# Attention ahead of two expert layers: k's maximum over slots in a PSUM bank, router columns with heads innermost, and a new order of tasks

## The chip, the cores and the metric

The kernel runs on one core of a Trainium2 chip. The core has five engines that take their instructions from queues of their own: TensorE (PE, the matrix engine), VectorE (DVE), ScalarE (ACT), GpSimd (POOL) and SyncE (SP, which here only issues DMAs). They share SBUF and the eight banks of PSUM, and meet through semaphores. The metric is the device time of one execution in microseconds, lower is better.

## What is computed

Linear attention over 8 batches of 8 heads, 576 positions and 64 columns, whose output is the input of two layers of experts (a top-1 router and eight experts each). The change touches the attention alone.

```python
def _attn_ref(q, k, v) -> np.ndarray:
    q_s = q - np.max(q, axis=-1, keepdims=True)
    q_s = np.exp(q_s)
    q_s = q_s / (np.sum(q_s, axis=-1, keepdims=True) + 1e-09)
    k_s = k - np.max(k, axis=2, keepdims=True)
    k_s = np.exp(k_s)
    k_s = k_s / (np.sum(k_s, axis=2, keepdims=True) + 1e-09)
    kv = np.einsum('bhsd,bhse->bhde', k_s, v)
    return np.einsum('bhsd,bhde->bhse', q_s, kv).astype(np.float32)

def reference(**kwargs):
...
    attn_out = _attn_ref(**attn_kwargs)
    B, H, S, D = attn_out.shape
    x = np.ascontiguousarray(attn_out.transpose(0, 2, 1, 3)).reshape(B * S, H * D)
    x = _moe_ref(x=x, **moe_kwargs)
    return _moe2_ref(x=x, **moe2_kwargs)
```

The maximum of k runs over the 576 positions, so it needs a maximum over slots on each partition and then one across partitions. Each expert layer sends a row of 512 to the expert with the largest logit; the first one leaves rows with a score of zero or less as they are.

## The kernel before

**Tiling.** The 576 positions of a batch are 512 in the main part, position 4p + j on partition p in slot j (NB = 4 slots), and 64 in a rest, which is slot 4 (NS = 5 slots). k lies in SBUF as `kt` [128, 8 heads, 5 slots, 64], two buffers for eight batches; v likewise as `vt`, q as `qt` with its rests as `qr` for two batches at a time.

**k's maximum** is made in `do_k` in two halves g of four heads. L191 (DVE) reduces over slots with the slot as the innermost index of a rearranged view, a step of 64 elements, and writes `m1`. PE transposes it into a bank of the pool `p1` (L193), DVE reduces over what were partitions (L195), ACT spreads the result to 128 columns (L196), PE transposes back into a second bank (L198). Then ek = k - maximum: on DVE straight from the bank in the batches listed under `kV` (L202), else on POOL from a copy that ACT makes (L204, L205). ACT takes the exponential (L206) and copies v beside a column of ones (`vp`, L207). PE multiplies (L216), which gives the product and the sum; L220 to L229 scale it into `KV`, on ACT in the batches of `nA`, else on DVE. L235 to L242 append to `KV` the 17 columns of the routers (8 and 8 logits and the score), so that the output and the routers' columns come out of one product.

**q and the output.** `do_q` subtracts each position's maximum (L251 on DVE; L252 on POOL, or on DVE in batches of `qV`) and takes the exponential. `do_out` transposes each slot (L270), multiplies by `KV` (L285), and DVE divides by the sum: the output into `xb` (L292), the 17 columns of each head into `lp` (L293), which lies as [slot, head, 17]. `place` sums `lp` over the heads (L314), finds the expert by some ten small DVE steps, counts places by PE (L325 to L327), and POOL scatters the rows to the array X in HBM (L344), 36 scatters in all. Eight batches make ten such units, the last two batches being cut in two.

**What sets the order.** Every piece is a task with a priority, a price for each engine that may run it, and the values it reads and writes (`sch.add`). `Order.emit` goes through time with these prices: it takes the ready task that can start first (within a window) and then by priority, gives it a buffer of its pool, and so writes a fixed order of instructions for every engine, the loads on SP among them. Priorities are batch x `step` plus an offset for the kind of task (`off`) and one for kind and batch (`ob`), from the table PRM. The pool `p1` has four PSUM banks, used for all transposes and small products; `po` has two.

**Behind it** the first expert layer splits its weights in two parts (L503 on ACT; L504 in turn on DVE and POOL) and runs its products at L534 and L564.

Of the kernel before, what the change touches and what calls it, by code (L numbers as in the profile page):

```python
# [94 lines left out]
def attention(tc,nc,raw,ctx,cst,q,k,v,routers,wgt,enD,X,accF,w1,w2,early,prm={}):  # L95
# [10 lines left out]
    def mk(name,shape,n,pool=None,dt=F32): pools[name]=[(pool or wk).tile(shape,dt,name=f"{name}{i}") for i in range(n)]  # L106
# [6 lines left out]
    mk('xb',[128,NS,XW],nb['xb'],raw); mk('lp',[128,NS,H,17],1)  # L113
# [67 lines left out]
    def do_k(b):  # L181
# [28 lines left out]
        for a in range(2):  # L210
# [19 lines left out]
            add(u+2*a+2,dict(A=1.0) if b in prm.get('nA',()) else dict(V=.5),f,[pk,ks],[(KV,a)])  # L230
        m=n; NC2=4//m
        for a in range(m):
# [10 lines left out]
            add(u+6,dict(A=.45) if b in prm.get('nA',()) else dict(V=.3),f,[p4],pt(KV,m,a))  # L243
    def do_q(b):
# [4 lines left out]
        for g in range(n):  # L249
            js=slice(NJ*g,NJ*g+NJ)  # L250
            add(u,dict(V=2.13/n+.07),lambda e,js=js: V.tensor_reduce(out=x.tile[:,:,js],in_=qt.tile[:,:,js],axis=AX.X,op=ALU.max),[qt],pt(x,n,g))  # L251
            add(u+.5,dict(V=2.13/n+.07) if fast else dict(P=4.4/n),lambda e,js=js: E[e].tensor_tensor(out=eq.tile[:,js].rearrange("p j h d -> p h j d"),in0=qt.tile[:,:,js],in1=x.tile[:,:,js].unsqueeze(3).to_broadcast([128,H,NJ,D]),op=ALU.subtract),[qt]+pt(x,n,g),pt(eq,n,g))  # L252
            add(u+1,dict(A=1.73/n+.07),lambda e,js=js: A.activation(out=eq.tile[:,js],in_=eq.tile[:,js],func=AF.Exp),[],pt(eq,n,g))
        if b%2:
            y=val(('qy',i))
            add(u,dict(V=.6),lambda e: V.tensor_reduce(out=y.tile,in_=qr.tile,axis=AX.X,op=ALU.max),[qr],[y])
            add(u+.5,dict(P=1.2),lambda e: P.tensor_tensor(out=qr.tile,in0=qr.tile,in1=y.tile.unsqueeze(2).to_broadcast([128,H,D]),op=ALU.subtract),[y],[qr])
            add(u+1,dict(A=.52),lambda e: A.activation(out=qr.tile,in_=qr.tile,func=AF.Exp),[],[qr])
    def do_out(b):
# [41 lines left out]
    def place(key,nj,xk,lk,xt,lt,prio,ids):  # L301
# [12 lines left out]
        add(prio,dict(V=.06+.145*nj),lambda e: V.tensor_reduce(out=l(),in_=lt().rearrange("p j h n -> p j n h"),axis=AX.X,op=ALU.add),lk,[ls])  # L314
# [543 lines left out]
```

## Time and profile before

| what | us |
|---|---|
| median of 3 runs (1058.69 to 1059.56) | 1058.87 |
| the profiled execution | 1061.93 |
| its span, first to last instruction | 1060.1 |
| attention, first instruction to the last DVE step of the routers' order | 0 to 176.0 |
| expert layers | from there to 1060.1 |

| engine, whole span | busy us | share |
|---|---|---|
| PE | 966.6 | 91% |
| DVE | 612.7 | 58% |
| ACT | 462.0 | 44% |
| POOL | 410.3 | 39% |

The shares are means over stages that have different limits: behind 176 us PE has the most work by far, in the attention PE and DVE are close. So the attention has to be read by itself: by the busy time in stretches, by the groups of instructions within 0 to 176.4 us, and by the waits. A group's row gives the source line, the engine, the operation, output and inputs by name, shapes, the count, the busy time in us and the mean duration in ns; after the bar the time that the engine stood idle just before them, and who ended it. Durations of one engine overlap a little where instructions follow each other without depending on each other, so that busy time is less than the sum of durations.

### The profile page before, as it was taken

How to read it: one execution, taken by the hardware profiler on the slowest of the kernel's cores; microseconds unless marked ns; L12 is line 12 of the kernel's file. 1: busy time of each engine (PE TensorE's matmuls, PEld its weight loads, DVE VectorE, ACT ScalarE, POOL GpSimd, SP SyncE). 2: the span in 40 equal slices, each digit the busy share in tenths (PEclk: the TensorE clock that was granted, in tenths of full speed). 3: DMA queues.
4: the chain of work that ended last, by engine and by line, in shares of the span. 5: the costliest groups of instructions: out<-in, count | busy, mean ns of one | idle time of the engine just before them, and what ended most of it. 6: DMA issues, size and time to landing. Idle time of an engine off the chain costs nothing. (4 is left out here: it accounts for less than half of the span.)

```text
span 1060.1 us, 19802 instructions
## 1 busy us (share of the span) xinstructions
PE 966.6 (91%) x6075; PEld 861.2 (81%) x6075; DVE 612.7 (58%) x1552; ACT 462.0 (44%) x945; POOL 410.3 (39%) x363
## 2 busy tenths in 40 slices
PE   4888987798899999999998899999999999999994
PEld 3777986786689977878996789889888899998893
DVE  6999877776466775766676621271634422255360
ACT  5877654125526252262225413273534332455352
POOL 6476846106958347273213711031401300134040
PEclk9999998899899999999999989999999999999998
DMA  9989725551653316233111372051341710063500
GB/s 289 317 249 321 251 95 208 194 182 41 226 165 113 119 62 204 89 121 123 49 54 54 120 265 72 32 205 58 117 142 40 250 43 22 22 217 114 171 29 22
DMA packets 88635, 144.76 MB, mean 137 GB/s; under 512 B 23439, under 2 KB 48015, under 8 KB 88288
## 3 DMA queue, kind: packets, MB, share of 16 engines
q1 hardware_dynamic: 78528, 115.42, 33.7%
q0 software_dynamic: 8640, 26.61, 6.6%
q8 instruction: 75, 1.23, 0.5%
q14 instruction: 144, 1.18, 0.4%
q10 hardware_dynamic: 1248, 0.32, 0.1%
HBM read 111.08 MB, written 33.68 MB: 137 GB/s over the span
## 5 line engine op out<-in xcount | busy, mean ns | idle before, releaser
L534 PE MATMUL P<-xT,w1h 128*128 128x256 f32 x1856 | 346.8, 289 | 5.6 <-ACT y L575 2.5
L564 PE MATMUL py<-w2h,hT 128*128 128x512 f32 x1072 | 344.8, 397 | 1.4 <-ACT ex L628 1.2
L534 PEld LDWEIGHTS P<-xT,w1h 128*128 128x128 f32 x1856 | 299.3, 197 | 8.8 <-issue 3.9
L534 PE MATMUL P<-xT,w1l 128*128 128x256 f32 x928 | 268.7, 290 | 10.3 <-DVE w1l L504 6.0
L564 PEld LDWEIGHTS py<-w2h,hT 128*128 128x128 f32 x1072 | 202.2, 189 | 46.9 <-DVE hT L511 3.7
L564 PE MATMUL py<-w2l,hT 128*128 128x512 f32 x536 | 211.8, 395 | 4.1 <-POOL w2l L504 3.0
L538 DVE SCALAR_TENSOR_TENSOR hT<-P,hT 128x512 fp32r<-128x512 f32 x116 | 77.6, 686 | 217.5 <-ACT hT L537 217.4
L534 PEld LDWEIGHTS P<-xT,w1l 128*128 128x128 f32 x928 | 182.9, 197 | 12.2 <-DVE w1l L504 6.3
L636 DVE SCALAR_TENSOR_TENSOR jk<-py,enB 128x512 bf16<-128x512 f32 x198 | 136.8, 691 | 24.3 <-ACT xb L572 10.7
L576 POOL DMA_INDIRECT out_dram<-y,idt x38 | 38.4, 1011 | 288.8 <-ACT y L575 236.5
L537 ACT ACTIVATE hT<-P 128x512 fp32r<-128x512 f32 x116 | 67.9, 595 | 183.8 <-PE P L534 179.1
L564 PEld LDWEIGHTS py<-w2l,hT 128*128 128x128 f32 x536 | 101.6, 190 | 31.3 <-POOL w2l L504 9.8
L504 POOL TENSOR_TENSOR w1l<-kt,w1h 128x512 fp32r<-128x512 f32 x64 | 83.8, 1340 | 59.7 <-ACT w1h L503 51.5
L504 POOL TENSOR_TENSOR w2l<-vt,w2h 128x512 fp32r<-128x512 f32 x76 | 101.2, 1360 | 1.4 <-ACT w2h L503 0.8
L575 ACT ACTIVATE y<-py,gate 128x512 f32<-128x512 f32 x38 | 26.0, 688 | 118.0 <-PE py L564 112.7
L503 ACT CAST w2h<-vt 128x512 fp32r<-128x512 f32 x104 | 55.5, 616 | 5.7 <-issue 4.2
L503 ACT CAST w1h<-kt 128x512 fp32r<-128x512 f32 x104 | 55.7, 638 | 0.8 <-DMA xb<-X 0.8
L572 ACT COPY xb<-py 128x512 f32<-128x512 f32 x17 | 10.0, 586 | 95.9 <-DVE flag L647 49.7
L511 DVE TENSOR_TENSOR hT<-P,hT 128x512 fp32r<-128x512 f32 x18 | 12.3, 686 | 63.8 <-ACT hT L510 63.8
L344 POOL DMA_INDIRECT X<-xb,pi x36 | 36.2, 1007 | 33.5 <-ACT pi L338 12.4
L635 POOL TENSOR_TENSOR pr<-xb,enB 128x512 f32<-128x512 f32 x20 | 25.4, 1291 | 60.0 <-ACT xb L572 60.0
L546 PE MATMUL P<-w1h,xT 128*128 128x512 f32 x144 | 47.4, 401 | 0.0
(242 smaller groups left out, 1334.8 us busy)
## 6 DMA issues: line engine op xcount, KB each, us to landing
vt<-in_moe_w_dram SPq DMA_DIRECT2D x26, 1024.0 KB
kt<-in_moe_w_dram SPq DMA_DIRECT2D x26, 1024.0 KB
xb<-X SPq DMA_DIRECT2D x56, 266.0 KB
kt<-in_k_dram SPq DMA_DIRECT2D x16, 512.0 KB
vt<-in_v_dram SPq DMA_DIRECT2D x16, 512.0 KB
qt<-in_q_dram SPq DMA_DIRECT2D x8, 1024.0 KB
xg<-X SPq DMA_DIRECT2D x28, 266.0 KB
X<-empty SPq DMA_DIRECT2D x16, 266.0 KB
```

Of the source, the lines that this page charges most:

```text
L344: i=P.indirect_dma_start(out=X,out_offset=IO(pi.tile[:,j:j+1]),in_=xt()[:,j],in_offset=None,bounds_check=ZROW,oob_is_err=False)
L503: nc.scalar.copy(h,a)
L504: (nc.gpsimd if lo[2*f+i]=='P' else nc.vector).tensor_tensor(out=l,in0=a,in1=h.bitcast(F32),op=ALU.subtract)
L534: T.matmul(o,lhsT=w[:,c,128*f:128*f+128],rhs=x[:,c],start=n==0,stop=n==11); n+=1
L537: A.activation(out=h,in_=q,func=AF.Relu)
L538: V.scalar_tensor_tensor(out=hl[:,f-1:f+1],in0=q,scalar=0.0,in1=h.bitcast(F32),op0=ALU.max,op1=ALU.subtract)
L546: T.matmul(self.P4[f],lhsT=x[:,c,0:128],rhs=w[:,c,512*f:512*f+512],start=n==0,stop=n==11); n+=1
L564: T.matmul(self.py[t],lhsT=x[:,c,a],rhs=w[:,c],start=n==0,stop=n==23); n+=1
L575: A.activation(out=y,in_=p,func=AF.Copy,scale=gt)
L576: P.indirect_dma_start(out=self.out,out_offset=IO(self.idt[:,i:i+1]),in_=y,in_offset=None,bounds_check=NTOK-1,oob_is_err=False)
L635: for e in range(n,8) if 'P' in eng else (): self.nc.gpsimd.tensor_tensor(out=self.pr[e-n],in0=x,in1=self.enB[:,e],op=ALU.mult)
L636: for e in range(n) if 'V' in eng else (): self.nc.vector.scalar_tensor_tensor(out=self.jk,in0=self.py[t],scalar=1.0,in1=self.enB[:,e],op0 ...
```

## The change

1. **k's maximum** is made for all eight heads at once, by L189 to L191 of the new file: ACT copies slot 0 into a bank of `p1`; DVE takes the maximum of the bank and slots 1, 2 and 3 in turn, each into the bank, and of the bank and slot 4 into `m1`. The transposes, the reduction (L197), the spread (L198) and ACT's copy (L202) come once for a batch, over 512 elements. The transposes go into the same bank.
2. **`lp`** lies as [slot, 17, head]: L297 writes each head's 17 columns with a step of eight elements, L318 reduces over neighbours.
3. **The table and the prices** are new: `step`, `off`, `ob`, and the lists `kV`, `qV` and `nA`, that is which batches have k's subtraction on DVE, q's on DVE, and KV's scaling on ACT. The instructions of every engine stand in a new order, SP's loads too.

Lines behind do_k stand four further down: L202 becomes L207, L227 L231, L251 L255, L285 L289, L292 L296, L293 L297, L314 L318, L344 L348, L504 L508.

```diff
-    mk('xb',[128,NS,XW],nb['xb'],raw); mk('lp',[128,NS,H,17],1)
+    mk('xb',[128,NS,XW],nb['xb'],raw); mk('lp',[128,NS,17,H],1)
...
+        p=val(('p1','a',b)); p2=val(('p1','b',b)); ks_=[(kt,0),(kt,1)]; acc=lambda: p.tile.rearrange("p (h d) -> p h d",d=D)
+        add(u-.5,dict(A=.5),lambda e: A.copy(acc(),kt.tile[:,:,0]),ks_,[p])
+        def fk(e,r):
+            for j in r: V.tensor_tensor(out=m1.tile if j==NB else acc(),in0=acc(),in1=kt.tile[:,:,j],op=ALU.max)
+        add(u,dict(V=1.22),lambda e: fk(e,(1,2)),ks_,[p])
+        add(u,dict(V=1.22),lambda e: fk(e,(3,4)),ks_+[(kt,2)],[p,m1])
+        def f1(e):
+            for c in range(4): T.transpose(p.tile[:,128*c:128*c+128],m1.tile[:,2*c:2*c+2].rearrange(hd),ident)
+        add(u+1,dict(T=.44),f1,[m1],[p])
+        add(u+1.5,dict(V=.61),lambda e: V.tensor_reduce(out=m2.tile,in_=p.tile.rearrange("p (c w) -> p c w",c=4),axis=AX.X,op=ALU.max),[p],[m2])
...
-            add(u,dict(V=1.40),lambda e,hs=hs: V.tensor_reduce(out=m1.tile[:,hs],in_=kt.tile[:,hs].rearrange("p h j d -> p h d j"),axis=AX.X,op=ALU.max),kp,pt(m1,n,g))
...
-            add(w+1,dict(V=.21),lambda e,po=po,rc=rc,lo=lo: V.tensor_tensor(out=lo().rearrange("p (c g) n -> p c g n",g=2),
...
+            add(w+1,dict(V=.21),lambda e,po=po,rc=rc,lo=lo: V.tensor_tensor(out=lo().rearrange("p n (c g) -> p c g n",g=2),
...
-        add(prio,dict(V=.06+.145*nj),lambda e: V.tensor_reduce(out=l(),in_=lt().rearrange("p j h n -> p j n h"),axis=AX.X,op=ALU.add),lk,[ls])
+        add(prio,dict(V=.06+.145*nj),lambda e: V.tensor_reduce(out=l(),in_=lt(),axis=AX.X,op=ALU.add),lk,[ls])
...
-PRM={
...
-'step': 10.171,
...
-'kV': (1, 6), 'qV': (2,), 'nA': (1, 2, 3, 6, 7),
...
+PRM={
...
+'step': 14.514,
...
+'kV': (1, 3, 7), 'qV': (), 'nA': (2, 3, 5),
...
```

The order that follows from it is shown at three places. First DVE at the very start, the maxima of batches 0 (`kt0`) and 1 (`kt1`); `m10` is `m1`, p11 and p12 are banks of `p1`. Before:

```order
L191 TENSOR_REDUCE m10_138<-kt0_126 128x256 x2
L195 TENSOR_REDUCE m20_139<-p11_181 128x2
L195 TENSOR_REDUCE m20_139<-p12_182 128x2
L191 TENSOR_REDUCE m10_138<-kt1_127 128x256 x2
L195 TENSOR_REDUCE m21_140<-p11_181 128x2
L195 TENSOR_REDUCE m21_140<-p12_182 128x2
L251 TENSOR_REDUCE qx0_151<-qt0_130 128x8x2
```

Each batch has two halves with a reduction (L195) for each, and q's reduction (L251) comes next. After:

```order
L191 TENSOR_TENSOR p11_181<-p11_181,kt0_126 128x512 x3
L191 TENSOR_TENSOR m10_138<-p11_181,kt0_126 128x512
L197 TENSOR_REDUCE m20_139<-p11_181 128x4
L191 TENSOR_TENSOR p12_182<-p12_182,kt1_127 128x512 x3
L191 TENSOR_TENSOR m10_138<-p12_182,kt1_127 128x512
L197 TENSOR_REDUCE m21_140<-p12_182 128x4
L207 TENSOR_TENSOR ek1_133<-kt1_127,p10_180 128x4x5x64 x2
L255 TENSOR_REDUCE qx0_151<-qt0_130 128x8x2 x2
```

The maxima follow each other as before, each now with four instructions and one reduction (L197), and batch 1's subtraction (L207) has moved ahead of q's reductions (L255), where L202 stood behind them.

Second DVE at batch 4, in the middle of the run; `pf`, `rc`, `lp` and `xb` belong to the routers' order and to outputs of other batches. Before:

```order
L291 RECIPROCAL rc1_165<-rc1_165 128x8
L191 TENSOR_REDUCE m10_138<-kt0_126 128x256 x2
L195 TENSOR_REDUCE m20_139<-p13_183 128x2
L293 TENSOR_TENSOR lp0_169<-po1_185,rc1_165 128x136
L292 TENSOR_TENSOR xb1_168<-po1_185,rc1_165 128x512
L195 TENSOR_REDUCE m20_139<-p10_180 128x2
```

Here the two halves stand together, and only one output comes between them and the last reduction. After:

```order
L191 TENSOR_TENSOR p13_183<-p13_183,kt1_127 128x512 x2
L340 TENSOR_REDUCE pf1_176<-p12_182 128x5
L294 TENSOR_SCALAR rc0_164<-po1_185 128x8
L191 TENSOR_TENSOR p13_183<-p13_183,kt1_127 128x512
L191 TENSOR_TENSOR m10_138<-p13_183,kt1_127 128x512
L295 RECIPROCAL rc0_164<-rc0_164 128x8
L294 TENSOR_SCALAR rc1_165<-po0_184 128x8
L297 TENSOR_TENSOR lp0_169<-po1_185,rc0_164 128x8x17
L296 TENSOR_TENSOR xb0_167<-po1_185,rc0_164 128x512
L295 RECIPROCAL rc1_165<-rc1_165 128x8
L197 TENSOR_REDUCE m20_139<-p13_183 128x4
```

Between the first maximum into bank p13 and the reduction L197, which frees it, seven other instructions stand.

Third the loads on SP behind those of k for batches 0 and 1. Before:

```order
L170 DMA vt0_128<-in_v_dram 64x8x64
L173 DMA vt0_128<-in_v_dram 128x4x256 x2
L178 DMA qt0_130<-in_q_dram 128x8x256
L170 DMA vt1_129<-in_v_dram 64x8x64
L173 DMA vt1_129<-in_v_dram 128x4x256 x2
L178 DMA qt1_131<-in_q_dram 128x8x256
```

v and q alternate. After:

```order
L170 DMA vt0_128<-in_v_dram 64x8x64
L173 DMA vt0_128<-in_v_dram 128x4x256 x2
L170 DMA vt1_129<-in_v_dram 64x8x64
L173 DMA vt1_129<-in_v_dram 128x4x256 x2
L178 DMA qt0_130<-in_q_dram 128x8x256
L178 DMA qt1_131<-in_q_dram 128x8x256
```

Two v tensors come ahead of the first q tensor. PE's first product takes `ek0` with `vp1`, so that batch 0's v is the second of the two:

```order
L200 MATMUL p10_180<-ident_60,m2b0_141 128x128 x4
L220 MATMUL p11_181<-vp1_135,ek0_132 128x130 x10
L220 MATMUL p13_183<-vp0_134,ek1_133 128x130 x5
L220 MATMUL p12_182<-vp1_135,ek0_132 128x130 x5
L220 MATMUL p13_183<-vp0_134,ek1_133 128x130 x5
```

In the kernel before, `ek0` was multiplied with `vp0`, the first v tensor.

## Rows read from the trace of the kernel before

**Rows 1.** Busy time by stretch: us, each engine's busy us (instructions), PE clock, DMA, GB/s.

```profile
8.90:20.00 11.10, 4.14 (x12) 1.74 (x12) 10.20 (x8) 5.21 (x8) 5.62 (x14) 1.00 1.11 349
20.00:140.00 120.00, 103.17 (x757) 96.42 (x758) 108.01 (x248) 88.18 (x168) 77.45 (x47) 0.94 0.90 278
140.00:164.00 24.00, 21.53 (x177) 20.33 (x176) 16.76 (x67) 12.30 (x41) 10.63 (x10) 1.00 0.27 103
...
0.00:176.40 176.40, 136.88 (x1006) 125.45 (x1006) 147.51 (x377) 112.30 (x232) 107.00 (x111) 0.95 0.79 246
```

**Rows 2.** PE's waits from 20 to 140 us: total us, times, longest.

```profile
PE p L193 <- DVE m L191: 4.6, 4, 1.5
PE p L216 <- DVE p L316: 2.8, 1, 2.8
PE po L285 <- DVE xb L292: 2.7, 2, 2.0
```

**Rows 3.** Busy time by stretch, three stretches of ten us.

```profile
70.00:80.00 10.00, 9.02 (x59) 8.17 (x59) 8.81 (x29) 7.56 (x16) 8.70 (x5) 0.83 0.91 279
...
110.00:120.00 10.00, 9.82 (x83) 9.56 (x81) 8.51 (x25) 7.18 (x11) 10.00 (x6) 1.00 0.71 227
...
130.00:140.00 10.00, 7.21 (x46) 7.00 (x45) 8.51 (x22) 4.99 (x10) 5.10 (x5) 0.83 0.49 167
```

**Rows 4.** Groups of DVE, 0 to 176.4 us: busy us, mean ns | idle before.

```profile
L191 DVE TENSOR_REDUCE m<-kt 128x256 f32<-128x1280 f32 x16 | 37.9, 2383 | 0.1
...
L292 DVE TENSOR_TENSOR xb<-po,rc 128x512 f32<-128x512 f32 x36 | 24.3, 678 | 0.1
...
L251 DVE TENSOR_REDUCE qx<-qt 128x16 f32<-128x1024 f32 x16 | 19.3, 1204 | 0.1
...
L293 DVE TENSOR_TENSOR lp<-po,rc 128x136 f32<-128x136 f32 x36 | 10.5, 293 | 0.4
...
L195 DVE TENSOR_REDUCE m<-p 128x2 f32<-128x256 f32 x16 | 6.5, 411 | 1.1 <-PE p L193 0.9
...
L202 DVE TENSOR_TENSOR ek<-kt,p 128x1280 f32<-128x1280 f32 x4 | 5.9, 1478 | 1.0 <-PE p L198 1.0
...
L252 DVE TENSOR_TENSOR eq<-qt,qx 128x1024 f32<-128x1024 f32 x2 | 4.8, 2381 | 0.0
...
L227 DVE TENSOR_TENSOR KV<-p,ks 64x128 f32<-64x128 f32 x12 | 3.4, 285 | 0.2
...
L242 DVE COPY KV<-p 64x34 f32<-64x34 f32 x12 | 2.2, 187 | 0.1
```

**Rows 5.** Busy time of line 314 alone in the attention.

```profile
0.00:176.40 176.40, 9.81 (x10) 0.95 0.79 246
```

**Rows 6.** Groups of DVE, 0 to 260 us: line 571, in the first expert layer.

```profile
L571 DVE SCALAR_TENSOR_TENSOR py<-py,gate,GE 128x512 f32<-128x512 f32 x4 | 3.0, 756 | 4.3 <-PE py L564 4.3
```

**Rows 7.** Groups of ACT, 0 to 176.4 us.

```profile
L280 ACT COPY eT<-p 128x512 f32<-128x512 f32 x32 | 18.3, 590 | 8.3 <-PE p L270 5.2 <-issue 1.1 <-remote 0.9
...
L229 ACT ACTIVATE KV<-p,ks 64x64 f32<-64x64 f32 x40 | 10.2, 302 | 6.1 <-DVE m L191 3.6 <-DVE rc L290 1.2 <-DVE ks L222 1.1
...
L196 ACT COPY m2b<-m 128x256 f32<-128x256 f32 x16 | 6.2, 402 | 11.7 <-DVE m L195 10.7 <-DVE xb L292 1.0
```

**Rows 8.** Groups of POOL, 0 to 176.4 us.

```profile
L205 POOL TENSOR_TENSOR ek<-kt,mb 128x1280 f32<-128x1280 f32 x12 | 34.8, 2910 | 24.3 <-ACT mb L204 18.9 <-DMA vt<-in_v_dram 5.0 <-POOL ek L205 0.3
...
L252 POOL TENSOR_TENSOR eq<-qt,qx 128x1024 f32<-128x1024 f32 x14 | 26.7, 1916 | 10.7 <-DVE p L321 4.6 <-DVE qx L251 4.2 <-DVE ks L222 1.9
```

**Rows 9.** Timeline: start, us, engine, line, operation [idle before <- releaser].

```profile
20.02 5.04 PE L216 MATMUL p<-vp,ek 128*128 128x130 f32 x30
...
175.85 0.19 DVE L336 TENSOR_REDUCE pf<-p 128x2 f32<-128x32 f32 x1
...
182.18 8.75 DVE L504 TENSOR_TENSOR w1l<-kt,w1h 128x512 fp32r<-128x512 f32 x1
...
190.98 0.58 PE L534 MATMUL P<-xT,w1l 128*128 128x256 f32 x1 [6.05 <-DVE w1l L504]
```

More of the change, by code (lines that the diff above doesn't have):

```diff
@@ new lines, in do_k, with f2 @@
+        add(u+1.5,dict(V=.61),lambda e: V.tensor_reduce(out=m2.tile,in_=p.tile.rearrange("p (c w) -> p c w",c=4),axis=AX.X,op=ALU.max),[p],[m2])
+        add(u+2,dict(A=.58),lambda e: A.copy(m2b.tile,m2.tile.unsqueeze(2).to_broadcast([128,4,128])),[m2],[m2b])
+        def f2(e):
+            for c in range(4): T.transpose(p2.tile[:,128*c:128*c+128],m2b.tile[:,c],ident)
+        add(u+2.5,dict(T=.44),f2,[m2b],[p2])
+        if not fast: add(u+3,dict(A=.5),lambda e: A.copy(mb.tile.rearrange(hd),p2.tile),[p2],[mb])
@@ L200, in do_k @@
+        for g in range(n):
+            hs=slice(NH*g,NH*g+NH); w=NC*128; kp=[(kt,g),(kt,2)]
             if fast:
-                add(u+3.5,dict(V=1.40),lambda e,hs=hs,p2=p2,w=w: V.tensor_tensor(out=ek.tile[:,:,hs].rearrange("p j h d -> p h j d"),in0=kt.tile[:,hs],in1=p2.tile[:,0:w].rearrange("p (h d) -> p h d",d=D).unsqueeze(2).to_broadcast([128,NH,NS,D]),op=ALU.subtract),kp+[p2],pt(ek,n,g))
+                add(u+3.5,dict(V=1.42),lambda e,hs=hs: V.tensor_tensor(out=ek.tile[:,:,hs].rearrange("p j h d -> p h j d"),in0=kt.tile[:,hs],in1=p2.tile.rearrange("p (h d) -> p h d",d=D)[:,hs].unsqueeze(2).to_broadcast([128,NH,NS,D]),op=ALU.subtract),kp+[p2],pt(ek,n,g))
@@ L207, in do_k @@
-            add(t0+at('v',b),dict(A=1.28),lambda e,hs=hs: A.copy(vp.tile[:,hs,:,0:D],vt.tile[:,hs]),[(vt,g),(vt,2)],pt(vp,n,g))
+                add(u+3.5,dict(P=2.87),lambda e,hs=hs: P.tensor_tensor(out=ek.tile[:,:,hs].rearrange("p j h d -> p h j d"),in0=kt.tile[:,hs],in1=mb.tile[:,hs].unsqueeze(2).to_broadcast([128,NH,NS,D]),op=ALU.subtract),kp+[mb],pt(ek,n,g))
+            add(u+4,dict(A=1.18),lambda e,hs=hs: A.activation(out=ek.tile[:,:,hs],in_=ek.tile[:,:,hs],func=AF.Exp),[],pt(ek,n,g))
+            add(t0+at('v',b),dict(A=1.18),lambda e,hs=hs: A.copy(vp.tile[:,hs,:,0:D],vt.tile[:,hs]),[(vt,g),(vt,2)],pt(vp,n,g))
@@ L251, in do_q @@
             add(u,dict(V=2.13/n+.07),lambda e,js=js: V.tensor_reduce(out=x.tile[:,:,js],in_=qt.tile[:,:,js],axis=AX.X,op=ALU.max),[qt],pt(x,n,g))
[L252 removed]
+            add(u+.5,dict(V=2.3) if fast else dict(P=3.8/n),lambda e,js=js: E[e].tensor_tensor(out=eq.tile[:,js].rearrange("p j h d -> p h j d"),in0=qt.tile[:,:,js],in1=x.tile[:,:,js].unsqueeze(3).to_broadcast([128,H,NJ,D]),op=ALU.subtract),[qt]+pt(x,n,g),pt(eq,n,g))
             add(u+1,dict(A=1.73/n+.07),lambda e,js=js: A.activation(out=eq.tile[:,js],in_=eq.tile[:,js],func=AF.Exp),[],pt(eq,n,g))
@@ L256, in do_q @@
             add(u,dict(V=.6),lambda e: V.tensor_reduce(out=y.tile,in_=qr.tile,axis=AX.X,op=ALU.max),[qr],[y])
-            add(u+.5,dict(P=1.2),lambda e: P.tensor_tensor(out=qr.tile,in0=qr.tile,in1=y.tile.unsqueeze(2).to_broadcast([128,H,D]),op=ALU.subtract),[y],[qr])
+            add(u+.5,dict(P=1.02),lambda e: P.tensor_tensor(out=qr.tile,in0=qr.tile,in1=y.tile.unsqueeze(2).to_broadcast([128,H,D]),op=ALU.subtract),[y],[qr])
             add(u+1,dict(A=.52),lambda e: A.activation(out=qr.tile,in_=qr.tile,func=AF.Exp),[],[qr])
```

30 lines of the change are left out of this document (8 added, 22 removed).

## The prediction

> **What bounds the kernel now.** The change touches only the attention, the part of the program ahead of the expert layers, so I read the trace by stages first. The view of busy time by stretch [rows 1] has one row for each stage: the filling from 8.9 to 20 us, the main run from 20 to 140, the run-out from 140, and the attention as a whole to 176.4. In the main run VectorE (DVE) is busy 108.0 of 120 us and TensorE (PE) 103.2: 90 and 86%. From 140 to 164 the picture turns: PE 21.5 of 24 us, DVE only 16.8. So two engines share the bound, DVE first, PE at the end, and what is won on DVE can be used only as far as PE follows.
>
> Who makes whom wait says which of the two leads. PE stands idle for 120 - 103.2 = 16.8 us of the main run, and the longest of its waits all end with DVE: for k's maximum (L191), for the small steps of the routers' order (L316), for the scaled output (L292) [rows 2]. These three alone are 10.1 us. ACT and POOL have 88 and 77 us of work in the same 120 [rows 1] and come later.
>
> The granted clock adds to it. Where PE had stood idle it was granted less: the two stretches of ten us with a mean of 0.83 [rows 3] (two more of the main run, from 80 and from 100 us, read the same) hold PE busy for 7.2 to 9.0 us, against 9.8 at full clock between 110 and 120. A mean of 0.83 over ten us is 3.4 us at 1.2 GHz instead of 2.4; four such stretches are 13.6 us in which PE's work took twice its time.
>
> **The change part by part.** Durations are those of the attention's groups [rows 4 to 8]; they are of the profiled execution, which took 1061.93 us (span 1060.1), 3.06 us over the median of 1058.87. The sum is made against 1061.93 and the 3.06 taken off at the end.
>
> *k's maximum, DVE.* Sixteen strided reductions of 2.383 us, 38.1 us in all, go [rows 4]. In their place stand 32 maxima of two operands over 512 elements, one operand in PSUM and one in SBUF. No such row exists in the trace. L292 reads PSUM and writes SBUF over 512 elements in 0.678 us [rows 4]; L571 works in place in PSUM with an SBUF operand, in 0.756 [rows 6]. L571 is nearer in its operands, but does two operations; I take 0.72, so 23.0 us and 15.1 saved, with 13.9 and 16.4 as ends. The reductions after the transposes become 8 over 512 elements instead of 16 of 0.411; at L251's 1.204 us for 1024 that is about 0.65 each, 5.2 for 6.6: 1.4 saved.
>
> *Work handed between engines.* The table lets DVE subtract k's maximum in three batches instead of two: two more halves of 1.478, +3.0. It takes q's subtraction of batch 2 off DVE: two of 2.381, -4.8. It moves the scaling of two more batches' KV from ACT to DVE: 8 rows of 0.285 and 8 of 0.187, +3.8 [rows 4]. POOL gets two of L252 at 1.916, +3.8, and gives up two of L205 at 2.910, -5.8 [rows 8]. ACT loses 16 rows of 0.302 (-4.8), gets 8 new copies of 512 elements, at L280's 0.590 (+4.7), and makes one broadcast copy of 512 instead of two of 0.402 for each batch (about -1.7) [rows 7]. So ACT and POOL both end a little lighter. PE's instructions stay the same in number and size; no DMA changes its size.
>
> *The routers' sums.* Ten reductions over h with a stride, 9.8 us [rows 5], read 36 x 136 = 4896 elements. In the new layout these lie side by side, as they do for L251, which needs 1.18 ns an element [rows 4]: 5.8 us, 4.0 saved. The price is paid by L297 (L293 before), 36 rows of 0.293: it now writes with a step of eight elements. A strided write has no row. Strided reading costs L191 1.86 ns an element against L251's 1.18, 0.68 more [rows 4]; by that the 136 elements would take 0.09 us more, 3.3 in all. A gain is excluded, since the elements and the PSUM reading stay as they were. I take half, 1.7, and keep 0 and 3.3.
>
> The Trainium skill (SBUF — State Buffer, section Door 1: The DMA port swizzle) says that SBUF answers at full rate only within 16-byte lines, so that fp32 elements further than four apart cost extra. The old reductions agree: 256 bytes apart and 1.86 ns. Its sentence names accesses, not reads alone; taken so it speaks against the new layout, whose writes lie 32 bytes apart, and DVE's saving would be 1.6 us smaller than the sum here: 1048 if DVE led to the end, 1044 if such writes cost nothing.
>
> DVE's sum: -15.1 - 1.4 + 3.0 - 4.8 + 3.8 - 4.0 + 1.7 = **-16.8 us** of 147.5, which leaves about 131; the ends are -14 and -20. PE, with 136.9 [rows 1], is then the longest.
>
> *How much PE can follow.* In the main run PE is busy 103.2 us, of which 13.6 at half clock. If PE waits less it stays at 2.4 GHz; at the run's busy share of 0.86, 13.6 x 0.86 / 2 = 5.8 us of it go, which leaves 97.4. How full can PE be? In the run-out, where DVE has slack, it reaches 21.5/24 = 0.90 [rows 1], between 110 and 120 us 0.98 [rows 3]. At 0.90 the main run takes 108.2 us, at 0.95 102.5. I take 0.91, next to the longer of the two rows: 107.0, **-13.0**. DVE then has 108.0 less its part of the 16.8 (some 14) = 94 in 107, 88%: close, but no longer ahead.
>
> *Filling and run-out.* The load queue (SP) now brings two v tensors before the first q, and the first of them is not that of batch 0: PE's first product for batch 0 (20.02 us now [rows 9]) needs one tensor more, 8 x 576 x 64 x 4 bytes = 1.18 MB, 3.4 us at 349 GB/s [rows 1]. It may start 0 to 3.4 us later; against that batch 1 is ready earlier, since its maximum stands next in DVE's row. I take +1. In the run-out half of the routers' saving falls where DVE's chain of small steps ends the attention (last step at 175.85 [rows 9]): -1. What was hidden and what is late next: the loads are far ahead, with a DMA share of 0.27 after 140 us [rows 1]; next late is PE itself, and behind it the long wait at the start of the expert layers, where L504 on DVE takes 8.75 us while POOL runs its own subtractions and PE waits 6.05 [rows 9]. Nothing in the change touches that order, so I let it move as a block. Everything from there on is the same program.
>
> Sum: 1061.93 - 13.0 + 1 - 1 = 1048.9; less 3.06, **1046 us**.
>
> **Rivals.**
> *Half the gain.* The waits for L191 go, but others take their place (routers' steps, scaled outputs), and PE's share stays at 0.86: 97.4 / 0.86 = 113.3, -6.7, so 1052. For it speaks that L316 and L292, which also release PE, stay [rows 2]; against it that they wait behind L191 in DVE's row now.
> *More.* PE reaches 0.95 (-17.5), and the new timing lets DVE finish its weight splitting ahead of POOL, so that the 6.05 us wait goes too: 1061.93 - 17.5 - 6.05 - 3.06 = 1035. Against it: POOL reaches its subtractions straight from the last scatters, as now.
> *Slower: the banks.* PE's transposes and products share four PSUM banks (p1). The new maximum keeps one from ACT's first copy to the reduction after the transposes. In batch 4 DVE's queue has 4 maxima (2.9 us) in that time and seven other instructions, the two longest of 0.29 and 0.68 [rows 4]; with the copy's 0.59 [rows 7] some 5 to 6 us, where a half batch holds one now for little more than its reduction of 0.411. If PE had to wait for a bank for 4 us more in each of 8 batches, 32 us stand against 13.0: 1059 + 19 = 1078. It decides from 1.6 us a batch. Against it: a batch now takes two holds for its maximum instead of four, and three banks stay in turn.
> *No gain.* DVE isn't what the end hangs on, and the main run is as long as its chain of batches: k loads wait for a free buffer, and this ends with the subtraction. Then 1059. Against it speak the waits [rows 2].
>
> **How the numbers follow.** PE-bound between 0.88 and 0.95: 0.60. Half the gain: 0.17. More: 0.07. No gain: 0.07. The banks: 0.09. So faster 0.84, same 0.07, slower 0.09, where 0.2% (2 us) is about what a measurement of this kernel tells from no change. The range reaches from 1038 (a main run at 0.95 and the whole 4.0 us of the routers' reductions won in the run-out: 1059 - 17.5 - 4) to 1056 (half the gain and a start later by 3.4: 1059 - 6.7 + 3.4). It leaves out no gain, the banks and most of the rival with more, some 0.2.
>
> **What would show it.** In the profile after: the new L191 at 0.68 to 0.76 us; L318 near 0.8 us for 680 elements; L297 between 0.29 and 0.39; DVE's total in the attention near 131 and PE's near 130 us, with PE's share in the middle over 0.90; waits of PE for L191 gone; the last DVE step of the attention near 163 instead of 176 us; the 8.75 us of L504 still there. The forecast is wrong if PE waits for ACT's first copy or for DVE's reduction L197 (a held bank), if a maximum takes over 1 us, or if the attention ends earlier and the expert layers give it back.

## Result

The changed kernel takes 1045.09 us (median of 4 runs, 1043.88 to 1047.01) where the kernel before takes 1059.21 (1058.69 to 1062.91): ratio 0.9861, 95% interval 0.9833 to 0.9888, so 1.4% faster. By this ratio it is 14.7 us; the medians are 14.1 us apart, and the two profiled executions, by which the terms below go, 16.3. Both kernels were run again beside the last experiments ("the last chip" below): 0.9860 (0.9837 to 0.9884). The kernel before against itself gave 0.9982 (0.9960 to 1.0003) there, which is what such a ratio is worth.

The forecast was 1046. The sum that led to it had one right part (the attention) and missed two large terms of opposite sign behind it, as the profile of after shows. First its busy time by stretch; columns as in [rows 1].

```profile
8.90:20.00 11.10, 3.38 (x13) 2.18 (x13) 6.95 (x11) 5.40 (x8) 4.04 (x14) 1.00 1.10 367
20.00:140.00 120.00, 109.53 (x850) 103.50 (x851) 101.81 (x288) 93.43 (x165) 81.94 (x51) 0.99 0.93 285
140.00:164.00 24.00, 17.79 (x142) 15.92 (x140) 19.81 (x95) 6.13 (x22) 10.47 (x11) 0.96 0.29 111
...
0.00:164.40 164.40, 131.26 (x1005) 122.10 (x1005) 130.46 (x401) 108.74 (x201) 104.19 (x111) 0.98 0.84 260
```

Against [rows 1] PE and DVE have changed places in the main run: PE 109.5 of 120 us (0.91), DVE 101.8. In the run-out it is DVE that is fuller now. The granted clock of the main run is 0.99 instead of 0.94. PE's waits of the main run (us in total, times, longest), to be held against [rows 2]:

```profile
PE p L220 <- ACT ek L210: 2.6, 1, 2.6
PE po L289 <- DVE xb L296: 2.4, 3, 1.4
PE p L200 <- ACT m2b L198: 1.5, 1, 1.5
PE p L195 <- DVE m L191: 1.4, 2, 1.2
```

The wait for k's maximum has fallen from 4.6 to 1.4 us, and none for ACT's first copy (L189) or the reduction L197, which would be a bank held by the maximum, is among PE's waits there. The groups of DVE in the attention, as in [rows 4]:

```profile
L296 DVE TENSOR_TENSOR xb<-po,rc 128x512 f32<-128x512 f32 x36 | 24.7, 685 | 0.0
...
L191 DVE TENSOR_TENSOR p<-p,kt 128x512 f32<-128x512 f32 x24 | 16.7, 694 | 1.2 <-ACT p L189 0.7
L297 DVE TENSOR_TENSOR lp<-po,rc 128x136 f32<-128x136 f32 x36 | 14.5, 404 | 0.4
L207 DVE TENSOR_TENSOR ek<-kt,p 128x1280 f32<-128x1280 f32 x6 | 8.8, 1478 | 2.1 <-PE p L200 1.9
...
L191 DVE TENSOR_TENSOR m<-p,kt 128x512 f32<-128x512 f32 x8 | 5.5, 691 | 0.3
L197 DVE TENSOR_REDUCE m<-p 128x4 f32<-128x512 f32 x8 | 5.3, 667 | 2.4 <-PE p L195 2.4
...
L318 DVE TENSOR_REDUCE ls<-lp 128x85 f32<-128x680 f32 x3 | 2.6, 856 | 0.0
```

A maximum takes 0.69 us, inside the bounds. L297 has gone from 0.293 to 0.404 us, 36 x 0.111 = 4.0 us more, past its upper bound of 0.39; all ten L318 together take 6.51 us instead of 9.81 [rows 5], 3.3 less. On DVE alone the new layout loses 0.7 us. The row of L318, as in [rows 5]:

```profile
0.00:176.40 176.40, 6.51 (x10) 0.95 0.83 258
```

Now the end of the attention and what follows, by the timeline (start, us, operation [idle before <- releaser]); the rows to compare are [rows 9].

```profile
23.72 0.58 PE L220 MATMUL p<-vp,ek 128*128 128x130 f32 x1 [2.63 <-ACT ek L210]
...
163.76 0.19 DVE L340 TENSOR_REDUCE pf<-p 128x2 f32<-128x32 f32 x1
168.42 1.09 PE L527 MATMUL pxT<-ident,GE 128*128 128x128 f32 x4 [4.93 <-DMA GE<-X]
...
171.70 0.67 DVE L508 TENSOR_TENSOR w1l<-kt,w1h 128x512 fp32r<-128x512 f32 x1
...
174.21 1.10 DVE L508 TENSOR_TENSOR w1l<-kt,w1h 128x512 fp32r<-128x512 f32 x1
176.74 3.24 DVE L508 TENSOR_TENSOR w1l<-kt,w1h 128x512 fp32r<-128x512 f32 x2
...
172.11 5.61 POOL L508 TENSOR_TENSOR w1l<-kt,w1h 128x512 fp32r<-128x512 f32 x4 [3.65 <-ACT w1h L507]
177.68 6.85 POOL L508 TENSOR_TENSOR w2l<-vt,w2h 128x512 fp32r<-128x512 f32 x4
```

The same passage in the kernel before, where [rows 9] do not show it:

```profile
176.36 1.12 PE L523 MATMUL pxT<-ident,GE 128*128 128x128 f32 x4 [0.79 <-ACT xb L339]
...
179.67 0.67 DVE L504 TENSOR_TENSOR w1l<-kt,w1h 128x512 fp32r<-128x512 f32 x1
...
180.48 5.01 POOL L504 TENSOR_TENSOR w1l<-kt,w1h 128x512 fp32r<-128x512 f32 x4
```

The last DVE step of the attention has moved from 175.85 to 163.76. Then PE stands for 4.93 us, since the first tokens (GE, read back from X) are not there; L523 before had no such wait. And the 8.75 us of DVE's second weight subtraction, for which PE waited 6.05, are gone: it takes 1.10. Those 8.75 us are called the block below.

The timelines of all runs give one table of that passage. E is the attention's last DVE step, T the first transposition of tokens (L523, L527), P the first product of the experts (L534, L538), Q the first one of their second half (L564, L568). From T to P all take 3.2 us.

| kernel | E, us | T - E | Q - P | span |
|---|---|---|---|---|
| before | 175.85 | 0.51 | 23.36 | 1060.1 |
| after | 163.76 | 4.66 | 15.64 | 1043.9 |
| before, last chip | 170.89 | 0.52 | 23.20 | 1054.5 |
| after, last chip | 164.04 | 4.89 | 15.62 | 1042.0 |
| form alone | 172.08 | 0.52 | 22.52 | 1054.1 |
| less DVE, old order | 171.29 | 0.52 | 23.06 | 1051.4 |
| time put back | 188.91 | 4.40 | 15.62 | 1067.2 |
| old layout | 167.01 | 4.58 | 15.63 | 1047.8 |
| rows written | 157.09 | 5.02 | 15.64 | 1039.8 |
| before, splits on DVE | 168.15 | 0.52 | 15.23 | 1040.7 |
| batch 6 first | 158.26 | 0.66 | 22.75 | 1037.5 |
| batch 6 first, splits on DVE | 158.47 | 0.53 | 14.77 | 1030.8 |
| after, splits on DVE | 163.05 | 4.93 | 14.77 | 1041.3 |
| all three | 164.86 | 0.52 | 14.77 | 1037.1 |

So the span's 16.2 us are: attention -12.1, the wait for GE +4.2, the weights -7.7, all the rest -0.6. On the last chip 12.5 are -6.9, +4.4, -7.6 and -2.4. Each is the difference of one profiled execution of either kernel.

### The profile page after: what moved, and what is told of

The parts are those of the page before. It is cut to its first block, busy times and chain, and to the rows that moved or that the text cites. A ratio compares the mean times of both kernels' runs of the same rounds, so it can differ in the third digit from the quotient of the medians.

```text
span 1043.9 us, 19789 instructions
## 1 busy us (share of the span) xinstructions
PE 958.6 (92%) x6075; PEld 854.5 (82%) x6075; DVE 593.0 (57%) x1576; ACT 458.8 (44%) x914; POOL 410.3 (39%) x363
## 5 line engine op out<-in xcount | busy, mean ns | idle before, releaser
L538 PE MATMUL P<-xT,w1h 128*128 128x256 f32 x1856 | 341.6, 286 | 5.5 <-ACTq L724 2.2
L568 PE MATMUL py<-w2h,hT 128*128 128x512 f32 x1072 | 344.8, 397 | 0.3
L538 PEld LDWEIGHTS P<-xT,w1h 128*128 128x128 f32 x1856 | 294.8, 194 | 8.7 <-issue 4.2
L538 PE MATMUL P<-xT,w1l 128*128 128x256 f32 x928 | 266.0, 287 | 4.5 <-POOL w1l L508 4.2
L568 PEld LDWEIGHTS py<-w2h,hT 128*128 128x128 f32 x1072 | 202.6, 190 | 45.6 <-DVE hT L515 3.7
L568 PE MATMUL py<-w2l,hT 128*128 128x512 f32 x536 | 212.3, 396 | 4.6 <-POOL w2l L508 3.5
L538 PEld LDWEIGHTS P<-xT,w1l 128*128 128x128 f32 x928 | 180.3, 194 | 6.3 <-POOL w1l L508 5.5
L568 PEld LDWEIGHTS py<-w2l,hT 128*128 128x128 f32 x536 | 101.5, 189 | 32.7 <-POOL w2l L508 11.2
L508 POOL TENSOR_TENSOR w1l<-kt,w1h 128x512 fp32r<-128x512 f32 x64 | 84.3, 1351 | 64.4 <-ACT w1h L507 64.2
L508 POOL TENSOR_TENSOR w2l<-vt,w2h 128x512 fp32r<-128x512 f32 x76 | 103.1, 1386 | 1.3 <-issue 0.7
L507 ACT CAST w2h<-vt 128x512 fp32r<-128x512 f32 x104 | 55.5, 616 | 5.8 <-issue 4.3
L507 ACT CAST w1h<-kt 128x512 fp32r<-128x512 f32 x104 | 55.7, 636 | 0.5 <-DMA xb<-X 0.5
L220 PE MATMUL p<-vp,ek 128*128 128x130 f32 x320 | 43.9, 291 | 3.5 <-ACT ek L210 2.6
```

The lines of the kernel that those rows point to most:

```text
L220: for j in range(NS): T.matmul(o,lhsT=ek.tile[:,j,2*c:2*c+2].rearrange(hd),rhs=vp.tile[:,2*c:2*c+2,j],start=j==0,stop=j==NB)
L507: nc.scalar.copy(h,a)
L508: (nc.gpsimd if lo[2*f+i]=='P' else nc.vector).tensor_tensor(out=l,in0=a,in1=h.bitcast(F32),op=ALU.subtract)
L538: T.matmul(o,lhsT=w[:,c,128*f:128*f+128],rhs=x[:,c],start=n==0,stop=n==11); n+=1
L568: T.matmul(self.py[t],lhsT=x[:,c,a],rhs=w[:,c],start=n==0,stop=n==23); n+=1
```

## Experiments

Theory T1: the gain is DVE's time in the main run, which PE was waiting for. Rival R1: it is the new order. Behind the attention: S1, DVE's weight subtraction is held by POOL's; G1, the wait for GE is for the tokens that batch 6 scatters last.

### DVE's time and the order, apart

**Form alone**: the kernel before with do_k exchanged, which brings the new maximum and the prices of do_k's own tasks; table, `kV`, `nA` and layout stay. The order is emitted anew from them.

```diff
-            add(u,dict(V=1.40),lambda e,hs=hs: V.tensor_reduce(out=m1.tile[:,hs],...
+        add(u-.5,dict(A=.5),lambda e: A.copy(acc(),kt.tile[:,:,0]),ks_,[p])
...
+            for j in r: V.tensor_tensor(out=m1.tile if j==NB else acc(),in0=acc(),in1=kt.tile[:,:,j],op=ALU.max)
...
```

> The kernel before with the new way of taking k's maximum alone (32 maxima of two operands in PSUM, one reduction and one broadcast copy for each batch); the table, the batches on DVE and the routers' layout stay the old ones. T1 (the end hangs on DVE's time in the main run): DVE loses some 17 us of its 147, PE has to follow, and the attention's last DVE step comes 7 to 12 us earlier than 175.8; time 1047 to 1052. R1 (the gain lies in the new table, not in the form): the old table was planned for the old form, the end stays within 2 us, 1057 to 1061. R2 (the held bank costs as much as the form saves): slower than 1060, with PE waiting for L195 or L200 in every batch.

Measured: 1054.32 us, ratio 0.9955 (0.9928 to 0.9982), 4.8 us (1.9 to 7.6); the median lies between the two expected ranges, in neither.

**Less DVE, old order**: three of five slots in the maximum.

```diff
-...in_=kt.tile[:,hs].rearrange("p h j d -> p h d j")...
+...in_=kt.tile[:,hs,0:3].rearrange("p h j d -> p h d j")...
```

> The kernel before, its order kept row by row, with k's maximum over three of the five slots (slots 3 and 4 are left out of the maximum; the softmax is the same for any shift that keeps the exponents in range). It takes 2/5 of 38.1 = 15 us off DVE and changes nothing else: no bank held, no copy on ACT, no new table. T1: the attention ends 7 to 12 us earlier, 1047 to 1052. R1 (order and table): 1057 to 1061. It also tells the price of the strided reduction by size: 768 elements at 1.86 ns are 1.43 us.

Measured: 1053.19 us, ratio 0.9939 (0.9911 to 0.9967). L191 took even less than expected:

```profile
L191 DVE TENSOR_REDUCE m<-kt 128x256 f32<-128x768 f32 x16 | 16.2, 1020 | 1.1 <-DMA kt<-in_k_dram 1.0
```

so that 37.9 - 16.2 = 21.7 us were off DVE, for 6.5 us of time by the ratio (3.5 to 9.4).

**Time put back**: the new kernel and order, 24 maxima done twice.

```diff
-            for j in r: V.tensor_tensor(...
+            for j in sorted(r+tuple(x for x in r if x<NB)): V.tensor_tensor(...
```

> The changed kernel, its order kept row by row, with 24 of the 32 maxima done twice (a maximum repeated changes nothing in the result), which puts 24 x 0.694 = 16.7 us back on DVE: the new order with about the old DVE time. T1 (the gain comes from DVE's time): attention's last DVE step goes from 163.8 back to 172 to 178, time 1053 to 1060. R1 (the gain comes from the new order): DVE has slack in it, the last step stays within 3 us of 163.8 and the time at 1045 to 1048.

Measured: 1065.48 us, ratio 1.0042 (1.0018 to 1.0066), above both expected ranges. Its main run and the first of its waits there:

```profile
20.00:140.00 120.00, 98.85 (x696) 92.98 (x697) 98.55 (x254) 85.56 (x152) 69.90 (x43) 0.91 0.82 254
```

```profile
PE p L195 <- DVE m L191: 11.6, 5, 3.2
```

PE falls from 109.5 to 98.9 us of 120, its clock from 0.99 to 0.91, and it waits 11.6 us for k's maximum: putting DVE's time back undoes the gain and more. So R1 in its plain form falls: the new order with the old time is slower than the kernel before, by 0.2 to 0.7%. The repeated maxima lengthen the way from k to its subtraction and the hold of the bank, too; that it is DVE's time as such, and not this way, that costs here, the run doesn't tell apart. R2 (the held bank) falls with the gain of the form alone. T1 holds in its direction but not in its size: in the old order 17 and 22 us less on DVE bring 4.8 and 6.5 us, not 7 to 12. DVE's busy time in the attention is 129.4 and 126.9 us there, less than the 130.5 of the changed kernel, and yet E is 172.08 and 171.29. The form alone shows where it stays (its stretches):

```profile
20.00:140.00 120.00, 108.11 (x809) 101.68 (x810) 98.02 (x269) 94.52 (x169) 84.76 (x51) 0.96 0.93 277
140.00:164.00 24.00, 21.15 (x165) 19.22 (x163) 15.52 (x68) 10.54 (x41) 8.08 (x9) 1.00 0.32 125
```

PE is busy for 108.1 us of the main run, but with 809 matmuls at a clock of 0.96, where the changed kernel has 850 at 0.99. So more of PE's work is left for the run-out, 21.2 of 24 us there against 17.8 in the new order, and DVE, which has slack now, waits for it: 8.7 us for PE between 140 and 173 us, against 3.0 between 140 and 164 in the changed kernel. Table and time belong together: by the middle of its interval neither the form alone nor the time alone gives half of the 14.7 us, though both intervals reach past it. The new table with the old form was not run.

### The routers' layout

**Old layout** in the changed kernel, order kept:

```diff
-...mk('lp',[128,NS,17,H],1)
+...mk('lp',[128,NS,H,17],1)
...
-...out=lo().rearrange("p n (c g) -> p c g n",g=2)...
+...out=lo().rearrange("p (c g) n -> p c g n",g=2)...
...
-...out=l(),in_=lt(),axis=AX.X...
+...out=l(),in_=lt().rearrange("p j h n -> p j n h"),axis=AX.X...
```

> The changed kernel, its order kept row by row, with the routers' columns laid out as before (h outside, n inside: L297 writes in a row, L318 reads with a step). By the prediction's sum the new layout is worth 4.0 - 1.7 = 2.3 us of DVE's time, so the old one would be 1 to 2.3 us slower: 1046 to 1048. By the rows of after (L297 36 x 0.111 us dearer, L318 only 3.3 us cheaper in sum) it is worth nothing: 1043.5 to 1046, the same within 1 us, unless the sums that stand at the attention's end count for more than their share, then 1 us slower.

Measured: 1049.16 us, ratio 0.9890 (0.9861 to 0.9920), above both expected ranges.

**Rows written**: new layout, L297 going through its elements in the order of SBUF:

```diff
-...out=lo().rearrange("p n (c g) -> p c g n",g=2),in0=po.tile[:,:,130:164].rearrange("p c (g n) -> p c g n",g=2),...[128,4,2,17]...
+...out=lo().rearrange("p n (c g) -> p n c g",g=2),in0=po.tile[:,:,130:164].rearrange("p c (g n) -> p n c g",g=2),...[128,17,4,2]...
```

> The changed kernel, its order kept row by row, with L297 going through its 136 elements in the order in which they lie in SBUF (columns outside, heads inside): it writes in a row and reads PSUM with a step. W1 (what costs is the strided write to SBUF): L297 goes back from 0.404 to about 0.29 us, DVE loses 36 x 0.11 = 4.0 us, the attention ends 1 to 3 us earlier, 1042 to 1044.5. W2 (any step costs, on whichever side): L297 stays at 0.39 us or more and the time within 1 us of 1045, or above.

Measured: 1042.51 us on a chip that gave the kernel before 1052.06, ratio 0.9908 (0.9886 to 0.9930). The rows of L297 and of the longest L318, first of the old layout, then of rows written:

```profile
L297 DVE TENSOR_TENSOR lp<-po,rc 128x136 f32<-128x136 f32 x36 | 10.6, 293 | 0.4
L318 DVE TENSOR_REDUCE ls<-lp 128x85 f32<-128x680 f32 x3 | 4.0, 1323 | 0.0
```

```profile
L297 DVE TENSOR_TENSOR lp<-po,rc 128x136 f32<-128x136 f32 x36 | 10.6, 293 | 0.4
L318 DVE TENSOR_REDUCE ls<-lp 128x85 f32<-128x680 f32 x3 | 2.6, 854 | 0.0
```

W1 holds for the instruction: the strided write to SBUF was the whole price, and reading PSUM with a step of 17 elements costs this instruction nothing. Rows written has the cheap form of both. In time the three layouts can't be told apart: the intervals of the old layout and of the changed kernel overlap, and on the chip of rows written the changed kernel was not run; against the 0.986 elsewhere its 0.9908 is no gain. That the layout is worth 2.3 us, as the prediction has it, is neither shown nor excluded.

### The start of the experts

**Before, splits on DVE**: all 16 subtractions of the weights' splits are given to DVE.

```diff
-self.split(0,(lambda: plan.heads(cst['base0'][:,0:8]),lambda: plan.rows(8*AREA,0,5)))
+self.split(0,(lambda: plan.heads(cst['base0'][:,0:8]),lambda: plan.rows(8*AREA,0,5)),'V'*8)
...
-self.split(1)
+self.split(1,(),'V'*8)
```

> The kernel before with all 16 subtractions that split the first experts' weights (L504 in the first start) on DVE instead of 8 on DVE and 8 on POOL; everything else is the same. S1 (DVE's second subtraction is held for 8.75 us because POOL's eight run without a gap): without POOL's the 16 take about 0.67 us each, PE's wait of 6.05 us for w1l goes, the first product with w1l starts 5 to 6 us earlier, 1053 to 1055 where the kernel before has 1059. S2 (it is DVE's own queue of small steps that PE waits for): the wait stays at 4 us or more, 1057 to 1060.

Measured: 1042.66 us against 1052.06, ratio 0.9914 (0.9894 to 0.9934): 9.1 us, more than the 6.05 of the wait. PE has no wait for w1l in its profile.

**Batch 6 first**: `'S6': 18.001` becomes `'S6': 10` in the table of the changed kernel.

> The changed kernel with one number of the table lowered (S6 from 18.0 to 10), by which batch 6's routers' steps on DVE stand ahead of batch 7's scaled outputs; its scatters should start 2 to 3 us earlier. G1 (L527's wait of 4.93 us is for the tokens that batch 6 scatters last): the wait shrinks to 2 to 3 us. G2 (the wait is the load's own time after the attention's end): it stays at 4 to 5. If the GE wait was also what kept ACT's copies behind POOL, so that POOL had gaps in which DVE's subtraction got through, then with a shorter wait POOL runs without gaps again, DVE's second L508 takes over 5 us and PE waits for w1l: 1044 to 1048, nothing won.

Measured: 1044.12 us against 1052.06, ratio 0.9929 (0.9909 to 0.9948); the changed kernel was not run on this chip, and against its 0.986 elsewhere nothing is won. The wait for GE went altogether, 0.66 us in the table, and with it the block came back:

```profile
158.92 1.09 PE L527 MATMUL pxT<-ident,GE 128*128 128x128 f32 x4 [0.93 <-ACT pi L342]
...
164.70 8.68 DVE L508 TENSOR_TENSOR w1l<-kt,w1h 128x512 fp32r<-128x512 f32 x1
```

**Batch 6 first, splits on DVE** has both edits.

> As the run with S6 at 10, and all 16 subtractions of the first experts' weights on DVE. If both mechanisms hold, the shorter wait for GE is kept and no w1l wait can come: L527 2 to 3 us earlier than 168.4, 1041 to 1043.5. If the wait for GE isn't batch 6's, or the splits on DVE hold up the hidden layer's L542 steps, within 1 us of 1045 or above.

Measured: 1033.24 us against 1052.06, ratio 0.9834 (0.9812 to 0.9857), 10.9 us below batch 6 first on the same chip. DVE's subtractions now follow at 0.6 us each:

```profile
162.30 1.27 DVE L508 TENSOR_TENSOR w1l<-kt,w1h 128x512 fp32r<-128x512 f32 x2
165.41 1.27 DVE L508 TENSOR_TENSOR w1l<-kt,w1h 128x512 fp32r<-128x512 f32 x2
```

**After, splits on DVE** has the splits alone, with S6 as it is.

> The changed kernel with the 16 subtractions of the first split all on DVE and S6 as it is. In the changed kernel PE doesn't wait for w1l any more (DVE's second L508 took 1.10 us), so by S1 there is nothing to win: within 2 us of the changed kernel, and L527 waits 4.9 us for GE as before. If POOL's subtractions cost more than that wait, 3 us or more faster.

Measured: 1043.12 us, ratio 0.9857 (0.9823 to 0.9892), where the changed kernel beside it has 0.9860: nothing to win, as S1 says where there is no block.

S1 and G1 hold in these runs. The last scatter of batch 6 starts 6.5 us ahead of E in the kernel before, 3.7 us in the changed one and 6.4 in batch 6 first (POOL's timelines, in this order):

```profile
169.35 0.98 POOL L344 DMA_INDIRECT X<-xb,pi  x1 [0.30 <-DVE xb L292]
```

```profile
160.11 0.98 POOL L348 DMA_INDIRECT X<-xb,pi  x1 [0.31 <-issue]
```

```profile
151.82 0.98 POOL L348 DMA_INDIRECT X<-xb,pi  x1 [0.30 <-issue]
```

From that start to PE's use of the tokens it is 8.3 us in the changed kernel (160.11 to 168.42) and was at most 7.0 (169.35 to 176.36), so 3.7 are too few. Why the way is at least 1.3 us longer was not tried. The rows show that the load of GE starts 3.4 us behind that scatter instead of 2.95, and that batch 7's scatters begin ahead of it in the changed kernel, behind it in the kernel before (first the kernel before, then the changed one):

```profile
172.30 0.88 SPq L367 DMA_DIRECT2D GE<-X  x2
...
174.12 0.98 POOL L344 DMA_INDIRECT X<-xb,pi  x1 [3.79 <-ACT pi L338]
```

```profile
162.04 0.98 POOL L348 DMA_INDIRECT X<-xb,pi  x1 [0.95 <-ACT pi L342]
...
163.51 0.92 SPq L371 DMA_DIRECT2D GE<-X  x2
```

And the two terms go together: with POOL's subtractions in place, the block is there in all five runs without a wait for GE and in none of the five with it. The wait holds ACT's weight copies (L507) too, so that POOL has to wait for them (3.65 us above). The two groups differ in one more thing: in the five with the block DVE's first subtraction is over when POOL's first starts (before: 179.67 + 0.67 against 180.48), in the other five it is still running (after: 171.70 + 0.67 against 172.11). What it is in that moment that lets DVE in was not tried apart.

### The two kernels again, and a faster one

> The kernel before, unchanged, profiled beside the next three on one chip. The chips of the last two comparisons gave it 1059.8 and 1052.1 us, and where it was faster the runs beside it were granted a mean of 0.99 to 1.00 in the main run instead of 0.94. C1 (the granted clock makes the difference between chips): a time near 1052 goes with 0.98 or more between 20 and 140 us, one near 1060 with 0.94 to 0.96, with the instructions' own durations unchanged. C2 (something else): the time and this clock do not go together.

> The changed kernel, unchanged, on the same chip. If the gain is DVE's time first (T1) and the clock only adds to it, the ratio is 0.985 to 0.989 where the kernel before is granted 0.94 to 0.96, and 0.989 to 0.994 where it is granted 0.98 or more, since there is no slow clock to win back. If the ratio is the same on both, the clock had no part in the gain.

Measured on one chip: before 1056.29 us in its ten runs (0.9982) and 1058.40 in the 17 that all four share; after 1044.51, ratio 0.9860. Main runs of before and of after:

```profile
20.00:140.00 120.00, 105.25 (x798) 98.19 (x799) 110.16 (x258) 91.17 (x175) 80.25 (x48) 0.97 0.89 278
```

```profile
20.00:140.00 120.00, 108.14 (x844) 101.68 (x845) 101.27 (x287) 93.34 (x165) 82.08 (x52) 0.99 0.94 287
```

At a clock of 0.97 the kernel before ends its attention at 170.89, 5 us earlier than in the profile of the prediction (0.94), while the changed one ends at 164.04 as before; so the attention's gain was 12.1 us there and is 6.9 here. The ratio is the same nevertheless. The two profiled executions of the kernel before lie 3.1 us above their median (1061.93, 1058.87) and 2.1 us below that of the 17 runs here (1056.26, 1058.40), so that a usual gain of the attention between the two is likely; the expectation's case of a clock of 0.98 or more did not occur, and what part the clock has in the gain stays open.

C1 is not borne out. Within this chip time and clock go together: the 17 runs of before go from 1052.20 us at a mean clock of 0.979 to 1063.70 at 0.968, which doesn't say which of the two follows from the other. Between chips they do not: at a mean clock of 0.973 or 0.974 over the whole run the kernel before took 1050.88 to 1053.27 us on the chip of batch 6 first, 1055.10 to 1058.93 here and 1058.79 to 1059.89 on the chip of the form alone. What makes the chips differ is open.

**All three**: rows written, S6 at 10, splits on DVE.

> The changed kernel with L297 written in a row, S6 at 10 and the 16 subtractions on DVE: the three edits that won something in the last comparison, together. If they are independent: the ratio to the kernel before is 0.979 to 0.982, 2 to 4 us below the run without L297's edit (0.9834). If L297's 4 us of DVE are taken up by PE's own work (PE 0.92 and more in the main run), the same as that run.

Measured: 1039.07 us, ratio 0.9812 (0.9783 to 0.9841): 5.4 us below the changed kernel and 19.3 below the kernel before on the same chip, with intervals that just touch the changed kernel's. The ratio stands 0.002 below the run without L297's edit, which is inside the intervals, and the attention ends no earlier than in the changed kernel (164.86, 164.04), though L297 is back at 0.295 us; what is plain to see is the passage to the experts, 0.52 instead of 4.89 and 14.77 instead of 15.62 us.

## Why the prediction came out right, step by step

- **What bounds.** DVE first, PE next: right, as far as the run with the time put back shows it.
- **k's maximum.** 0.694 and 0.691 against 0.72, L197 0.667 against 0.65. DVE in the attention 130.5 us against 131, PE 131.3 against 130.
- **PE's share.** 0.913 against 0.91; the main run's gain and clock came as the sum had them in that pair of profiles: E 163.76 against "near 163". But 6.4 us of the forecast's 13.0 were the return from a low clock (5.8 us of busy time at a share of 0.91), and how much low clock there is to win back differs between executions of before: 0.94 in that profile, 0.97 on the last chip, where the attention gave 6.9. So the agreement of this step is in part luck.
- **That DVE's time alone would do it.** The sum takes 16.8 us off DVE and lets PE follow, whatever the order. In the old order that much off DVE is worth 4.8 us in the form alone; the sum was right only because the new table came with it.
- **The layout.** Mis-sized: L297 0.404 us, outside the bound from the strided reads, and L318 0.856 for 680 elements, 3.3 us won in place of 4.0. The step "I take half" was wrong; the sentence on 16-byte lines (the Trainium skill, SBUF — State Buffer, section Door 1: The DMA port swizzle) had the better side: rows written shows that the writes carry the price.
- **Filling.** Mis-sized, and not for the reason given: PE's first product starts at 23.72 instead of 20.02, 3.7 us later where +1 was taken and 3.4 was the bound. Its wait ends with ACT's exponential (L210), not with a load of v. In the form alone, whose loads of v and q still alternate, it starts at 22.50, so that 2.5 of the 3.7 us come without the new loads; POOL's first subtraction, which needs the maximum of all eight heads now, starts there at 17.01 us instead of 15.43. E came near the forecast all the same; what made up for it is not shown.
- **The start of the experts.** Wrong: "Nothing in the change touches that order, so I let it move as a block." The order did not change, but its times did: batch 6's scatters came closer to the attention's end, the load of GE stuck out by 4.2 us, and the 7.7 us of the block went with it; the sign "the 8.75 us of L504 still there" did not come. Net -3.5 us that the sum does not have. On the last chip they make up for half of what the attention gave less than forecast, so that the number came out right partly for a reason that was not its own, by luck.
- **Rivals.** More: its vanished wait for w1l came, but through ACT and GE, not through a faster DVE, and PE's share stayed at 0.91. Banks: no wait of PE for one that the maximum holds. Half the gain and no gain: excluded by the interval, though for the attention alone half the gain (-6.7) is what the profiles of the last chip showed.

## To carry to other kernels

Time taken off an engine turns into an earlier end only with an order planned for the new time; run the form alone and the order with the old time put back to see how much each holds. When a stage is forecast to move earlier "as a block", list what each of its first instructions waits for and how many microseconds of cover each has: a load that just came in time no longer does when its producers move by less than the end. And cost a stall by the distance between two fixed points behind it, not by the wait alone.

## What the hardware showed unexpectedly

- **A run of POOL instructions holds one of DVE's.** On the last chip DVE's second subtraction in the kernel before took 8.72 us, from 177.22 to 185.94, while POOL ran its eight at 1.24 each up to 185.40:

```profile
177.22 8.72 DVE L504 TENSOR_TENSOR w1l<-kt,w1h 128x512 fp32r<-128x512 f32 x1
...
175.51 5.00 POOL L504 TENSOR_TENSOR w1l<-kt,w1h 128x512 fp32r<-128x512 f32 x4
180.47 4.93 POOL L504 TENSOR_TENSOR w2l<-vt,w2h 128x512 fp32r<-128x512 f32 x4
```

  In the changed kernel the two alternate, each 1.7 us after its last (POOL at 177.68, 179.39 and 181.09, DVE at 178.19, 179.90 and 181.60). The Trainium skill (SBUF — State Buffer, section SBUF: two separate sides) says that a DVE operation with two inputs in SBUF and a GpSimd operation that reads SBUF share a port pair, which the first to start keeps for the whole instruction. The alternation agrees with that; that one DVE instruction waited for several of POOL's in a row goes beyond it.
- **The stall costs more than its wait.** Where the block came and went, PE had waited 5.1 to 6.2 us for it (5.08 in batch 6 first, 6.18 on the last chip); Q - P fell by 7.6 to 8.1. Behind the wait PE is busy without a gap, but granted less at first. In the kernel before on the last chip it waits from 179.82 to 186.00; from 186 to 192 the granted clock is 0.52, almost all at the lower level of 1.2 GHz, and from 192 on 1.00. Its stretches:

```profile
180.00:188.00 8.00, 2.00 (x9) 2.00 (x10) 7.86 (x14) 2.93 (x7) 5.40 (x5) 0.81 0.46 176
188.00:196.00 8.00, 8.00 (x55) 8.00 (x54) 5.37 (x12) 1.19 (x2) 0.00 (x0) 0.76 0.64 265
196.00:204.00 8.00, 8.00 (x45) 6.94 (x45) 5.87 (x21) 1.57 (x3) 0.00 (x0) 1.00 0.72 204
```

- **A write in steps of 32 bytes** costs L297 0.404 us for 136 elements instead of 0.293; a PSUM read in steps of 17 elements costs nothing there.
- **The strided reduction** costs 1.020 us for 768 elements (three slots), 1.33 ns an element, but 2.383 for 1280 (five), 1.86. Its price can't be scaled by the number of elements.
